# The start of a retention and feed-forward kernel: v scaled by ScalarE, weight conversion behind the rows, fewer warm-up matmuls

## The chip, the cores and the metric

The kernel runs on one core of a Trainium2 chip. Its time is device time of that core in microseconds (us), the median of several runs of the same program. The trace is one more execution, taken by the hardware profiler. TensorE does the matmuls, VectorE and ScalarE elementwise work, GpSimd (POOL in the rows) a few tensor operations, SyncE (SP) issues nearly all transfers.

## The reference

A retention layer and a feed-forward layer, in float32:

```python
state = zeros(B, H, D, D)                     # B 4, H 8, S 768, D 64
for t in range(S):
    state = gamma * state + k[t] (outer) v[t] # gamma: one decay per head
    y[t] = scale * q[t] @ state
x = y as (3072 tokens, 512)
h = x @ w_in                                  # 512 x 2048
g = h * clip(h + 3, 0, 6) / 6
out = g @ w_out                               # 2048 x 512
```

## The kernel before

**Tiling.** The 3072 tokens are 24 row slices (`NROW`) of 128 tokens, six per batch; four slices (`UR`) make a unit of 512 tokens, so there are six units. The recurrence over t is done in slices: scores k·q of a slice, masked to be causal, times v, plus the running state times q. The decay is taken out by scaling v with one constant per token and head (`cst_sb`) and y with its reciprocal (`dq`).

**A row burst** (`burst(r)`) is one visit of that part. On TensorE: `y` of slice r-1 from the state (L218), scores `sc` of slice r (L225), `y` of slice r-1 from the masked scores (L229), running sum `uz` of slice r (L253). On VectorE: `xr` (y times decay, L244), the mask `am` of the scores (L266). On ScalarE: the copy `state` of `uz` (L262). Then `x`, the feed-forward input, is split into a high half (ScalarE, L127) and a low half (VectorE, L128), since a product is made of three reduced-precision matmuls high·high, high·low, low·high. The score bank, the `y` bank and the mask tile exist once, so bursts follow each other closely: the next scores wait for the mask, the next `y` for `xr`.

**Weights.** w_in and w_out come as 64-bit words and are turned into float32 by integer operations (`to_f32`, L99 to L124): L109, L110, L115, L118, L121 on VectorE and L113 on ScalarE, 512 columns at a time, and then the same split in two halves. A staging tile `st` exists twice; the other temporaries (`we`, `wb`, `ww`) once. In `attention()` the first eight slices (`AHEAD`) are loaded ahead, and after slices 0, 1, 4 and 7 (`WITH`) one of 16 w_in blocks is loaded and converted (`build_w1`). Blocks 4 to 15 follow later, one per product.

**Products.** `mm1(u, jj)` computes 12 matmuls `h` (L309), then `g` on ScalarE (L313) and VectorE (L314), which goes to HBM. The steps run through unit 0 with unit 1 between, then units 2 to 5; between the first products the next bursts stand. After that the second product (L395) reads `g` back.

**What sets the order.** All engines run their instructions in the order in which they stand. On TensorE that order is written out in the program (`tc.manual_schedule`). On the others a scheduler places instructions by readiness and by where they stand in the program text, so moving a call moves its instructions on VectorE, ScalarE and SyncE's transfer queue. Eight transfers are under way at a time; a ninth waits for the first to land.

**The start.** `WARM` = 24 matmuls on a zero tile run first (L170). The table that ScalarE needs for its functions is loaded ahead of its first activation, that of the first conversion. v of a slice is scaled by one GpSimd instruction (L196), which waits for v to land.

Of the kernel before, what the change touches and what calls it, by code (L numbers as in the profile page):

```python
# [9 lines left out]
F32 = mybir.dt.float32  # L10
# [3 lines left out]
I64 = mybir.dt.int64  # L14
AF = mybir.ActivationFunctionType
ALU = mybir.AluOpType
# [3 lines left out]
P = 128  # L20
# [9 lines left out]
def retention_ffn(ctx: ExitStack, tc: tile.TileContext, qkv, w_in, w_out, dvs, dqs, out, B, H, S, D):  # L30
# [6 lines left out]
    nc = tc.nc  # L37
# [4 lines left out]
    NK = DM // P  # L42
# [3 lines left out]
    UT = UR * P  # L46
    NU = NROW // UR
    HM = DM // 2
    WARM = 24
    AHEAD = 2 * UR  # L50
    WITH = (0, 1, 4, 7)
    BUFS = {"lkt": 1, "lqt": 2, "lvn": 2, "lkn": 1}
    SPARE = ("lkn", "lkt", "lqt", "lqt")
    BLK = 2 * P
# [19 lines left out]
    )  # L74
    ebias = const.tile([P, 1], F32, name="ebias")
    nc.gpsimd.memset(ebias, -896.0 * 2**23)
    serial = iter(range(1 << 30))

    def nm(s):
        return f"{s}_{next(serial)}"  # L80
# [15 lines left out]
    ps_a = att.enter_context(tc.tile_pool(name="ps_a", bufs=1, space=PSUM, side="right"))  # L96


    def to_f32(src):  # L99

        n = src.shape[-1]
        st = wst.tile([P, n], I64, tag="st", name=nm("st"), bufs=2)
        b = wst.tile([P, n], I32, tag="wb", name=nm("wb"))
        e = wst.tile([P, n], I32, tag="we", name=nm("we"))
        w = wst.tile([P, n], F32, tag="ww", name=nm("ww"))
        nc.sync.dma_start(out=st, in_=src)
        words = st.bitcast(I32).rearrange("p (n w) -> p n w", w=2)
        lo, hi = words[:, :, 0], words[:, :, 1]
        nc.vector.tensor_scalar(out=e, in0=hi, scalar1=0x7FF00000, scalar2=None, op0=ALU.bitwise_and)  # L109
        nc.vector.tensor_scalar(  # L110
            out=b, in0=hi, scalar1=0xFFFFF, scalar2=0x100000, op0=ALU.bitwise_and, op1=ALU.bitwise_or
        )
        nc.scalar.activation(out=e, in_=e, func=AF.Relu, scale=8.0, bias=ebias)  # L113
        y = b.bitcast(F32)
        nc.vector.scalar_tensor_tensor(  # L115
            out=y, in0=lo.bitcast(U32), scalar=2.0**-32, in1=b, op0=ALU.mult, op1=ALU.add
        )
        nc.vector.scalar_tensor_tensor(  # L118
            out=e, in0=hi, scalar=-2147483648, in1=e, op0=ALU.bitwise_and, op1=ALU.bitwise_or
        )  # L120
        nc.vector.scalar_tensor_tensor(  # L121
            out=w, in0=y, scalar=2.0**-20, in1=e.bitcast(F32), op0=ALU.mult, op1=ALU.mult
        )
        return w  # L124
# [11 lines left out]
            w1s[s] = wpool.tile([P, 14, 2, P], F32R, tag="w", name=nm("w1"))  # L136
        return w1s[s], o

    def build_w1(j):
        w = to_f32(w_in[j]).rearrange("p (k n) -> p k n", k=NK)  # L140
        k = 0
        while k < NK:
            t, o = w1_block(j, k)
            n = min(NK - k, 14 - o)
            split(t[:, o : o + n, 0], t[:, o : o + n, 1], w[:, k : k + n])
            k += n
# [4 lines left out]
    def build_w2(n):  # L151
        j, h = divmod(n, 2)
        if not h:
            w2c[j] = wpool.tile([P, 7, 2, 2, P], F32R, tag="w", name=nm("w2"))
        w = to_f32(w_out[j, h]).rearrange("p (b n) -> p b n", b=4)
        sm = wst.tile([P, 4, P], F32, tag="ws", name=nm("ws"))
        m12, m11, m21, m22 = (w[:, i] for i in range(4))
        dve_sub(sm[:, 1], m12, m11)
        dve_sub(sm[:, 2], m22, sm[:, 1])
        dve_sub(sm[:, 3], m22, m12)  # L160
        dve_sub(sm[:, 0], sm[:, 2], m21)
        split(w2c[j][:, 0:3, 0, h], w2c[j][:, 0:3, 1, h], w[:, 1:4])
        split(w2c[j][:, 3:7, 0, h], w2c[j][:, 3:7, 1, h], sm)
# [14 lines left out]
    def load(r):  # L178

        t = rows[r] = {}
        if r < AHEAD and r % 2 == 0:
            early[r] = wpool.tile([P, 7, NPAIR, P], F32, tag="w", name=nm("early"))
        for i, (x, n) in enumerate((("kt", 1), ("qt", 0), ("vn", 3), ("kn", 2))):
            o = r % 2 * 4 + i
            if r < AHEAD and o < 7:
                t[x] = early[r // 2 * 2][:, o]
            else:  # L190
                tag = SPARE[r // 2] if r < AHEAD else f"l{x}"
                t[x] = apool.tile([P, NPAIR, P], F32, tag=tag, name=nm(x), bufs=BUFS[tag])
            if x != "kn" or r % ROWS_B < ROWS_B - 1:
                nc.sync.dma_start(out=t[x].rearrange("p h n -> p (h n)"), in_=qkv[r, n])
        v = t["vn"].rearrange("p a (h e) -> p (a h) e", h=2)
        nc.gpsimd.tensor_tensor(  # L196
            out=v, in0=v, in1=cst_sb[:, r % ROWS_B, :, None].to_broadcast([P, H, D]), op=ALU.mult
        )

    def load_decay(r):  # L200
        if r < AHEAD:
# [70 lines left out]

    def attention():

        for r in range(AHEAD):
            load(r)
            load_decay(r)
            if r in WITH:
                build_w1(WITH.index(r))
        for r in range(NROW + 1):  # L280
            if r == AHEAD:
                burst(r, new=False)
                yield
                burst(r, old=False)
            else:
                burst(r)
            if r >= AHEAD - 1 and r + 1 < NROW:
                load(r + 1)
            if AHEAD <= r < NROW:
                load_decay(r)  # L290
            yield
# [194 lines left out]
```

## Time and profile before

| | |
|---|---|
| median of 3 runs | 618.72 us (616.77 to 618.96) |
| profiled execution | 617.5 us, its span 615.8 us |
| TensorE busy | 598.9 us (97%) |
| VectorE busy | 459.6 us (75%) |
| ScalarE busy | 242.0 us (39%) |
| GpSimd busy | 26.2 us (4%) |
| mean granted TensorE clock | 0.989 |

The span runs from the first to the last instruction of the trace; the profiled time includes what lies around it. A share of the span is an average: TensorE's 97% says nothing of the first 43 us, in which it works 31.56 us. So the front has to be read from timelines, in which a row is one instruction or several equal ones in a row: its start, its time, the engine, the line, output and inputs by the program's names, their shapes, the count, and in brackets how long the engine had nothing to do before it and what ended that. A float32 matmul stands as two records there: 48 for the 24 of the warm-up. The granted clock is 1.00 at TensorE's full 2.4 GHz and 0.50 at 1.2 GHz.

### The profile page before, as it was taken

To read this page: it belongs to the slowest core of one execution; us is meant where nothing else is said; L and a number is where in the kernel's file an instruction comes from. 1 tells how busy PE (TensorE), PEld (TensorE's weight loads), DVE (VectorE), ACT (ScalarE), POOL (GpSimd) and SP (SyncE) were. 2 spreads that over 40 slices of the span, in tenths; PEclk is the share of its full clock that TensorE was granted. 3 is DMA by queue.
4 is the path that set the end of the run, shared out by engine and by line. 5 is a ranking of instruction groups with operands and counts; after the bars stand their busy time and mean duration, and the time that the engine had idled before them with its cause. 6 is when DMAs were issued, how large, how long until landed. Compare 5 with 4: busy or idle time off the path is not lost.

```text
span 615.8 us, 11512 instructions
## 1 busy us (share of the span) xinstructions
PE 598.9 (97%) x4464; PEld 541.1 (88%) x4464; DVE 459.6 (75%) x960; ACT 242.0 (39%) x475; POOL 26.2 (4%) x32
## 2 busy tenths in 40 slices
PE   7779999999999999999999999999999999999997
PEld 7658788888788888888888889999999999999997
DVE  4669999999633399333335997988998889888993
ACT  2224454453322253222223554444444444444441
POOL 1301000000000100000000000000000000000000
PEclk9779999999999999999999999999999999999999
DMA  8936577765754457544425435434443444434421
GB/s 325 388 126 211 189 256 237 236 213 174 251 215 157 157 187 238 189 155 155 154 85 188 139 119 188 137 106 141 146 147 117 134 137 137 138 103 137 138 70 35
DMA packets 64726, 104.06 MB, mean 169 GB/s; under 512 B 5792, under 2 KB 30880, under 8 KB 64672
## 3 DMA queue, kind: packets, MB, share of 16 engines
q1 hardware_dynamic: 64528, 103.31, 49.8%
q8 instruction: 35, 0.57, 0.4%
q14 instruction: 19, 0.16, 0.1%
q10 hardware_dynamic: 144, 0.02, 0.0%
HBM read 71.85 MB, written 31.46 MB: 168 GB/s over the span
## 4 chain that ended last, share of the span: by engine, by line
PE 78%; DVE 18%; issue 3%; ACT 1%; DMA 0%; DVEq 0%; ACTq 0%
PE o L395 39%; PE h L309 30%; PE sc L225 3%; DVE g L314 3%; PE y L229 2%; DVE we L118 2%; DVE am L266 2%; DVE wb L115 2%; DVE w L128 2%; PE y L218 2%; DVE ww L121 2%; PE idle L170 1%; DVE x L128 1%; DVE we L109 1%; DVE xr L244 1%
## 5 line engine op out<-in xcount | busy, mean ns | idle before, releaser
L309 PE MATMUL h<-x,w 128*128 128x512 f32 x1152 | 271.6, 395 | 5.6 <-ACT x L127 4.2
L309 PEld LDWEIGHTS h<-x,w 128*128 128x128 f32 x1152 | 215.9, 189 | 53.9 <-ACT x L127 4.8
L395 PEld LDWEIGHTS o<-w,gc 128*128 128x128 f32 x2016 | 239.4, 190 | 0.1
L395 PE MATMUL o<-w,gc 128*128 128x256 f32 x2016 | 239.5, 281 | 0.0
L314 DVE SCALAR_TENSOR_TENSOR g<-g,h 128x512 f32<-128x512 f32 x96 | 65.6, 684 | 89.7 <-ACT g L313 89.7
L313 ACT ACTIVATE g<-h,three 128x512 f32<-128x512 f32 x96 | 65.6, 685 | 110.4 <-PE h L309 105.8
L127 ACT ACTIVATE gc<-gr 128x256 fp32r<-128x256 f32 x144 | 49.6, 407 | 117.2 <-PE o L395 113.9
L128 DVE TENSOR_TENSOR gc<-gr,gc 128x256 fp32r<-128x256 f32 x144 | 52.7, 420 | 19.7 <-ACT gc L127 19.6
L128 DVE TENSOR_TENSOR gc<-gsum,gc 128x768 fp32r<-128x768 f32 x96 | 62.0, 688 | 5.6 <-ACT gc L127 5.6
L127 ACT ACTIVATE gc<-gsum 128x768 fp32r<-128x768 f32 x96 | 54.5, 616 | 0.1
L127 ACT ACTIVATE w<-ww 128x384 fp32r<-128x384 f32 (+2 forms) x34 | 18.7, 555 | 50.2 <-DVE ww L121 45.1
L113 ACT ACTIVATE we<-we,ebias 128x512 int32<-128x512 int32 x32 | 22.9, 717 | 16.8 <-DVE we L109 16.8
L266 DVE TENSOR_TENSOR am<-sc,mask 128x1024 f32<-128x1024 f32 x24 | 29.2, 1215 | 0.4 <-PE sc L225 0.4
L196 POOL TENSOR_TENSOR vn<-vn,cst_sb 128x512 f32<-128x512 f32 x16 | 16.9, 1059 | 250.3 <-DMA vn<-in_qkv 250.3
L121 DVE SCALAR_TENSOR_TENSOR ww<-wb,we 128x512 f32<-128x512 f32 x32 | 24.3, 758 | 0.7
L118 DVE SCALAR_TENSOR_TENSOR we<-st,we 128x512 int32<-128x512 int32 x32 | 24.0, 750 | 0.0
L262 ACT ACTIVATE state<-uz 128x512 f32<-128x512 f32 x20 | 11.8, 590 | 27.6 <-PE uz L253 27.6
L128 DVE TENSOR_TENSOR w<-ww,w 128x384 fp32r<-128x384 f32 (+2 forms) x34 | 20.2, 598 | 2.8 <-ACT w L127 2.8
L115 DVE SCALAR_TENSOR_TENSOR wb<-st,wb 128x512 f32<-128x512 uint32 x32 | 22.0, 686 | 0.2
L86 DVE TENSOR_TENSOR gsum<-gr 128x256 f32<-128x256 f32 x48 | 20.4, 424 | 1.7 <-DMA gr<-gd 0.3
L83 DVE TENSOR_TENSOR gsum<-gr,gsum 128x256 f32<-128x256 f32 x48 | 20.2, 421 | 0.7
L244 DVE TENSOR_TENSOR xr<-y,dq 128x512 f32<-128x512 f32 x16 | 11.0, 688 | 12.5 <-PE y L229 12.5
(49 smaller groups left out, 379.2 us busy)
## 6 DMA issues: line engine op xcount, KB each, us to landing
gd<-g SPq DMA_DIRECT2D x96, 256.0 KB, 2.1
gr<-gd SPq DMA_DIRECT2D x96, 256.0 KB, 3.1
st<-in_w_in SPq DMA_DIRECT2D x16, 512.0 KB, 3.7
st<-in_w_out SPq DMA_DIRECT2D x16, 512.0 KB, 3.8
early<-in_qkv SPq DMA_DIRECT2D x28, 256.0 KB, 6.0
out<-ot SPq DMA_DIRECT2D x11, 512.0 KB, 2.8
kn<-in_qkv SPq DMA_DIRECT2D x16, 256.0 KB, 4.9
kt<-in_qkv SPq DMA_DIRECT2D x16, 256.0 KB, 4.5
```

The source lines that it names most:

```text
L86: nc.vector.tensor_tensor(out=out_, in0=a, in1=b, op=ALU.add)
L113: nc.scalar.activation(out=e, in_=e, func=AF.Relu, scale=8.0, bias=ebias)
L115: nc.vector.scalar_tensor_tensor(out=y, in0=lo.bitcast(U32), scalar=2.0**-32, in1=b, op0=ALU.mult, op1=ALU.add)
L118: nc.vector.scalar_tensor_tensor(out=e, in0=hi, scalar=-2147483648, in1=e, op0=ALU.bitwise_and, op1=ALU.bitwise_or)
L121: nc.vector.scalar_tensor_tensor(out=w, in0=y, scalar=2.0**-20, in1=e.bitcast(F32), op0=ALU.mult, op1=ALU.mult)
L127: nc.scalar.activation(out=hi, in_=src, func=AF.Copy)
L128: nc.vector.tensor_tensor(out=lo, in0=src, in1=hi, op=ALU.subtract)
L266: nc.vector.tensor_tensor(out=new["am"].rearrange("p h a n -> p (h a) n"), in0=sc.rearrange("p h a n -> p (h a) n"), in1=mask[:, None, :]. ...
L309: nc.tensor.matmul(h, t[:, o, a], xs[u][b][:, k], start=k + n == 0, stop=(k, n) == (NK - 1, 2), skip_group_check=True)
L313: nc.scalar.activation(out=g, in_=h, func=AF.Relu, bias=three)
L314: ins = nc.vector.scalar_tensor_tensor(out=g, in0=g, scalar=6.0, in1=h, op0=ALU.min, op1=ALU.mult)
L395: nc.tensor.matmul(ps, gc[:, a, LEFT[i], jj, :], wc[:, RIGHT[i], b_], start=first and j == 0 and n == 0, stop=j == NFP - 1 and n == 2, ski ...
```

## The change

Four things change, all in the first part of the program:

- `WARM` goes from 24 to 14.
- A one-column activation on ScalarE stands at the start, so that its table load does too.
- For the first eight slices v is scaled by ScalarE, with eight instructions of 64 columns (one per head), instead of one GpSimd instruction of 512. Later slices stay on GpSimd.
- Loading and converting a w_in block are parted (`fetch`, `to_f32`). The first four blocks are fetched after slices 0, 2, 3 and 5 and converted behind the bursts of slices 0, 2, 3 and 4.

```diff
-    WARM = 24
+    WARM = 14
     AHEAD = 2 * UR
-    WITH = (0, 1, 4, 7)
+    WITH = (0, 2, 3, 5)
...
+    table = const.tile([P, 1], F32, name="table")
+    nc.scalar.activation(out=table, in_=three, func=AF.Relu, bias=three)
...
-    def to_f32(src):
-        n = src.shape[-1]
-        st = wst.tile([P, n], I64, tag="st", name=nm("st"), bufs=2)
+    def fetch(src):
+        st = wst.tile([P, src.shape[-1]], I64, tag="st", name=nm("st"), bufs=2)
+        nc.sync.dma_start(out=st, in_=src)
+        return st
+    def to_f32(st):
+        n = st.shape[-1]
         b = wst.tile([P, n], I32, tag="wb", name=nm("wb"))
         e = wst.tile([P, n], I32, tag="we", name=nm("we"))
         w = wst.tile([P, n], F32, tag="ww", name=nm("ww"))
-        nc.sync.dma_start(out=st, in_=src)
...
-    def build_w1(j):
-        w = to_f32(w_in[j]).rearrange("p (k n) -> p k n", k=NK)
+    def build_w1(j, st=None):
+        w = to_f32(fetch(w_in[j]) if st is None else st).rearrange("p (k n) -> p k n", k=NK)
...
-        nc.gpsimd.tensor_tensor(
-            out=v, in0=v, in1=cst_sb[:, r % ROWS_B, :, None].to_broadcast([P, H, D]), op=ALU.mult
-        )
+        if r < AHEAD:
+            for h in range(H):
+                nc.scalar.activation(
+                    out=v[:, h], in_=v[:, h], func=AF.Copy, scale=cst_sb[:, r % ROWS_B, h : h + 1]
+                )
+        else:
+            nc.gpsimd.tensor_tensor(
+                out=v, in0=v, in1=cst_sb[:, r % ROWS_B, :, None].to_broadcast([P, H, D]), op=ALU.mult
+            )
...
+        st = []
         for r in range(AHEAD):
             load(r)
             load_decay(r)
             if r in WITH:
-                build_w1(WITH.index(r))
+                st.append(fetch(w_in[len(st)]))
         for r in range(NROW + 1):
...
                 burst(r)
+            if st and r in (0, 2, 3, 4):
+                build_w1(len(WITH) - len(st), st.pop(0))
```

VectorE's first twelve instructions behind the two memsets, in the kernel before (L109 to L121: conversion, `w1` L128: low half of weights, `am` L266: mask, `xr` L244 and `x` L128: a slice's output and its low half):

```order
L109 TENSOR_SCALAR we_4_139<-st_2_137 128x512
L110 TENSOR_SCALAR wb_3_138<-st_2_137 128x512
L115 SCALAR_TENSOR_TENSOR wb_3_138<-st_2_137,wb_3_138 128x512
L266 TENSOR_TENSOR am_29_258<-sc_27_239,mask_75 128x1024
L118 SCALAR_TENSOR_TENSOR we_4_139<-st_2_137,we_4_139 128x512
L121 SCALAR_TENSOR_TENSOR ww_5_140<-wb_3_138,we_4_139 128x512
L128 TENSOR_TENSOR w1_6_148<-ww_5_140,w1_6_148 128x4x128
L109 TENSOR_SCALAR we_10_160<-st_8_158 128x512
L110 TENSOR_SCALAR wb_9_159<-st_8_158 128x512
L244 TENSOR_TENSOR xr_33_279<-y_30_260,early_1_135 128x512
L115 SCALAR_TENSOR_TENSOR wb_9_159<-st_8_158,wb_9_159 128x512
L118 SCALAR_TENSOR_TENSOR we_10_160<-st_8_158,we_10_160 128x512
```

The same place in the changed kernel (lines 6 to 15 higher: mask L278, `xr` L256, low halves L134, conversion L115 to L127):

```order
L115 TENSOR_SCALAR we_17_261<-st_2_136 128x512
L278 TENSOR_TENSOR am_15_258<-sc_13_239,mask_75 128x1024
L116 TENSOR_SCALAR wb_16_260<-st_2_136 128x512
L124 SCALAR_TENSOR_TENSOR we_17_261<-st_2_136,we_17_261 128x512
L121 SCALAR_TENSOR_TENSOR wb_16_260<-st_2_136,wb_16_260 128x512
L127 SCALAR_TENSOR_TENSOR ww_18_262<-wb_16_260,we_17_261 128x512
L256 TENSOR_TENSOR xr_23_291<-y_20_272,early_1_134 128x512
L278 TENSOR_TENSOR am_25_305<-sc_21_273,mask_75 128x1024
L134 TENSOR_TENSOR x_22_290<-xr_23_291,x_22_290 128x4x128
L256 TENSOR_TENSOR xr_28_329<-y_26_307,early_1_134 128x512
L278 TENSOR_TENSOR am_30_343<-sc_27_312,mask_75 128x1024
L134 TENSOR_TENSOR x_22_290<-xr_28_329,x_22_290 128x4x128
```

The mask now stands behind the conversion's first instruction instead of its third, the second conversion has left this place for the two following slices, and the low half of the first weights has gone behind the fourth `x`. One instruction of the first conversion is still ahead of every mask.

ScalarE ahead of the first product, in the kernel before (`state` L262, high halves L127, `we` of a conversion L113, first `g` L313):

```order
L127 ACTIVATE x_32_278<-xr_43_355 128x4x128
L113 ACTIVATE we_17_194<-we_17_194,ebias_78 128x512
L127 ACTIVATE w1_6_148<-ww_18_195 128x4x128
L262 ACTIVATE state_49_405<-uz_125 128x512
L127 ACTIVATE x_32_278<-xr_48_393 128x4x128
L313 ACTIVATE g_52_422<-h_51_409,three_73 128x512
```

In the changed kernel (`state` L274, high halves L133, `we` L119, scaling of v L204, of slices 5 and 6 here):

```order
L274 ACTIVATE state_45_439<-uz_117 128x512
L133 ACTIVATE x_22_290<-xr_44_427 128x4x128
L204 ACTIVATE early_8_184<-early_8_184,cst_sb_71 128x64 x8
L133 ACTIVATE w1_19_269<-ww_18_262 128x4x128
L133 ACTIVATE w1_19_269<-ww_33_347 128x4x128
L119 ACTIVATE we_40_395<-we_40_395,ebias_78 128x512
L204 ACTIVATE early_11_213<-early_11_213,cst_sb_71 128x64 x8
L133 ACTIVATE w1_19_269<-ww_41_396 128x4x128
```

The high half of the first weights, which the first `h` reads, now stands behind the fourth `x` and the eight instructions that wait for v of slice 5; those of the second and third weights follow it.

## Rows read from the trace of the kernel before

**Rows 1.** Stages: length, busy us (count) per engine, PEclk, DMA share, GB/s.
```profile
70.00:158.00 88.00, 87.90 (x556) 73.22 (x554) 86.90 (x168) 43.50 (x73) 3.26 (x3) 1.00 0.67 226
158.00:612.00 454.00, 453.71 (x3375) 418.82 (x3375) 321.69 (x714) 176.09 (x366) 11.60 (x11) 1.00 0.44 146
```

**Rows 2.** TensorE's timeline: start, us, instruction, count, idle before and releaser.
```profile
1.25 7.58 PE L170 MATMUL idle<-warm 128*128 128x128 f32 x48 [1.25 <-DVE warm L167]
...
11.32 1.16 PE L225 MATMUL sc<-early 64*128 64x128 f32 x16 [0.79 <-DVE am L266]
...
20.09 2.08 PE L225 MATMUL sc<-early 64*128 64x128 f32 x16 [3.23 <-DVE am L266]
...
27.50 1.09 PE L229 MATMUL y<-am,early 128*64 128x128 f32 x16
...
36.81 0.79 PE L309 MATMUL h<-x,w 128*128 128x512 f32 x1 [3.64 <-ACT x L127]
38.08 5.02 PE L309 MATMUL h<-x,w 128*128 128x512 f32 x11 [0.47 <-DVE x L128]
...
46.03 3.02 PE L309 MATMUL h<-x,w 128*128 128x512 f32 x12
...
67.81 2.79 PE L309 MATMUL h<-x,w 128*128 128x512 f32 x11 [0.50 <-DVE x L128]
```

**Rows 3.** VectorE's timeline, 8 to 68 us.
```profile
8.15 0.43 DVE L109 TENSOR_SCALAR we<-st 128x512 int32<-128x512 int32 x1 [6.36 <-DMA st<-in_w_in]
...
10.04 1.23 DVE L266 TENSOR_TENSOR am<-sc,mask 128x1024 f32<-128x1024 f32 x1 [0.40 <-PE sc L225]
11.18 1.08 DVE L118 SCALAR_TENSOR_TENSOR we<-st,we 128x512 int32<-128x512 int32 x1
...
13.68 0.69 DVE L128 TENSOR_TENSOR w<-ww,w 128x512 fp32r<-128x512 f32 x1 [0.70 <-ACT w L127]
...
24.12 0.69 DVE L244 TENSOR_TENSOR xr<-y,early 128x512 f32<-128x512 f32 x1 [3.25 <-PE y L229]
...
28.64 0.69 DVE L244 TENSOR_TENSOR xr<-y,early 128x512 f32<-128x512 f32 x1 [1.77 <-PE y L229]
...
32.84 1.53 DVE L118 SCALAR_TENSOR_TENSOR we<-st,we 128x512 int32<-128x512 int32 x1
...
43.85 0.69 DVE L314 SCALAR_TENSOR_TENSOR g<-g,h 128x512 f32<-128x512 f32 x1 [5.83 <-ACT g L313]
...
45.86 0.69 DVE L118 SCALAR_TENSOR_TENSOR we<-st,we 128x512 int32<-128x512 int32 x1
...
67.07 0.68 DVE L128 TENSOR_TENSOR x<-xr,x 128x512 fp32r<-128x512 f32 x1
```

**Rows 4.** GpSimd's timeline: scaling of v.
```profile
5.69 1.04 POOL L196 TENSOR_TENSOR early<-early,cst_sb 128x512 f32<-128x512 f32 x1 [4.29 <-DMA early<-in_qkv]
10.67 1.04 POOL L196 TENSOR_TENSOR early<-early,cst_sb 128x512 f32<-128x512 f32 x1 [3.94 <-DMA early<-in_qkv]
...
32.75 1.06 POOL L196 TENSOR_TENSOR early<-early,cst_sb 128x512 f32<-128x512 f32 x1 [1.66 <-DMA early<-in_qkv]
```

**Rows 5.** ScalarE's groups by form, whole run: busy us, mean ns, idle before.
```profile
L127 ACT ACTIVATE gc<-gr 128x256 fp32r<-128x256 f32 x144 | 49.6, 407 | 117.2 <-PE o L395 113.9 <-DMA gr<-gd 3.4
L127 ACT ACTIVATE gc<-gsum 128x768 fp32r<-128x768 f32 x48 | 39.9, 831 | 0.1
L113 ACT ACTIVATE we<-we,ebias 128x512 int32<-128x512 int32 x32 | 22.9, 717 | 16.8 <-DVE we L109 16.8
...
L127 ACT ACTIVATE w<-ww 128x512 fp32r<-128x512 f32 x14 | 8.8, 632 | 23.7 <-DVE ww L121 21.0 <-issue 2.6
```

**Rows 6.** ScalarE's timeline: table load, two copies in a row.
```profile
8.66 1.28 ACT L113 ACT_TABLE_LOAD   x1 [8.66 <-DVE we L109]
...
47.30 0.73 ACT L127 ACTIVATE w<-ww 128x256 fp32r<-128x256 f32 x2 [1.67 <-DVE ww L121]
```

**Rows 7.** One stage of the front, columns as in rows 1.
```profile
20.00:24.00 4.00, 3.91 (x36) 3.69 (x38) 0.87 (x2) 0.00 (x0) 1.36 (x2) 0.50 1.05 394
```

More of the change, by code (lines that the diff above doesn't have):

```diff
@@ L154, in build_w2 @@
             w2c[j] = wpool.tile([P, 7, 2, 2, P], F32R, tag="w", name=nm("w2"))
-        w = to_f32(w_out[j, h]).rearrange("p (b n) -> p b n", b=4)
+        w = to_f32(fetch(w_out[j, h])).rearrange("p (b n) -> p b n", b=4)
         sm = wst.tile([P, 4, P], F32, tag="ws", name=nm("ws"))
```

## Prediction

> **What bounds the kernel now.** I read the stage table first. From 70 to 158 us TensorE is busy 87.90 of 88.00 us, from there to 612 us 453.71 of 454.00 [rows 1]: however the front is ordered, the matmuls behind it run without a hole, so time can only come from when that stream starts. VectorE is full from 70 to 158 us too (86.90 of 88.00). So a lead at 70 us lasts to the end only if both engines have it: the smaller of the two counts.
>
> TensorE's timeline shows the stream's start [rows 2]: 24 warm-up matmuls hold the engine from 1.25 to 8.83 us, row bursts with holes follow, the first product `h` starts at 36.81 us (after 3.64 us without work) and goes on at 38.08, and a last hole ends at 67.81, where a low half of `x` is awaited from VectorE. VectorE's timeline says why [rows 3]: its first conversion waits for `w_in` until 8.15 us; idle times of 0.40, 0.70, 3.25, 1.77 and 5.83 us follow, the last for the first `g`; and the fourth `x` low half of the second unit, the one TensorE waits for, begins at 67.07 and ends at 67.75. That end is the milestone that I work with.
>
> A second loss hides in VectorE's busy time. `L118` takes 0.69 us undisturbed; at 11.18 it took 1.08 and at 32.84 it took 1.53, each time ending about 0.55 us after a GpSimd scaling of v that had begun at 10.67 and 32.75 [rows 3, 4]. These are the first and the last of five such instructions from 8 to 38 us; with the three between them (16.16, 19.96 and 30.38 us) the excesses are 0.39, 0.84, 0.23, 0.57 and 0.84, together 2.9 us.
>
> **The change, part by part.** Up to the milestone VectorE executes the same instructions, in another order. From 8.15 to 67.75 are 59.6 us; less 11.95 us of the idle above and 2.9 us of blocking, 44.7 us of work remain. The milestone's new time is 8.15 + 44.7 + what the new order leaves idle, so I walk through that order.
>
> *Warm-up.* 14 of 24 at the old mean is 14/24 x 7.58 = 4.4 us: the end moves from 8.83 to 5.7 us. The first scores need `kt` and `qt`, which are queued ahead of v, and v had landed when GpSimd took it at 5.69 [rows 4]; so they run from 5.7 to 6.9. That alone gives little: VectorE's new first instruction still waits for `w_in` until 8.15, and the first mask stands behind it, at 8.5 instead of 10.04.
>
> *Scaling of v.* Eight ScalarE instructions of 128x64 per row, which no row shows. A copy of 128x256 takes 407 ns and one of 128x768 831 ns, so 0.83 ns a column, and 64 columns make 248 ns [rows 5]. The form with a bias read from memory takes 717 against 632 ns for 512 columns, 85 ns more; I add that for the scale read from memory: 0.33 us. Two copies in a row took 0.73 us for 2 x 0.41, an overlap of 0.09 [rows 6]. Eight are 8 x 0.33 - 7 x 0.09 = 2.0 us. Lower end: without the 85 ns, 1.35 us. Upper end: each as long as the 128x256 copy, without overlap, 3.3 us. I take 2.0, since each part of it is a measured difference; GpSimd needed 1.04. The Trainium skill, "ScalarE: Activation LUTs", section "What ACT_TABLE_LOAD costs", gives 186 ns + 0.833 ns per column, 93 ns more for a pointer operand and 93 ns of overlap; by that the eight would take 2.0 us, and the sum would stay.
>
> *Table.* Its load took 1.28 us from 8.66 [rows 6], while VectorE had its own second and third instruction to do; now it is over before v lands. I put it at 0: the activation behind it now waits for VectorE's first instruction (8.5) and is done by 9.7, and its result is asked for at 10.0.
>
> *Transfers.* They go on at about 390 GB/s [rows 7], 0.67 us for a tile of 256 KB and 1.3 for 512 KB. From v of row 1 at 10.67, by the new order of the queue: v of row 2 at 14.0, row 3 at 18.7, row 4 at 23.3, row 5 at 26.7, row 6 at 30.7, row 7 at 33.4. The third and fourth `w_in` wait for a staging buffer inside the queue, now ahead of more rows; VectorE frees these at about 11.3 and 22.0, before the queue gets there (about 15 and 22.6). So the price is nothing, and each microsecond that the second is late beyond 0.6 delays rows 6 and 7 by one.
>
> *Rows 0 to 4.* A row's cycle is scores 1.16, y 1.09, xr 0.69, mask 1.23 us, less overlaps, about 4.05 [rows 2, 3]. `xr` of row 0 at 12.0. ScalarE scales v of row 1 until 12.65, the state sums end at 13.3, scores of row 2 start at 14.3; `xr` of row 1 at 16.45 (before 24.12), of row 2 at 20.45 (before 28.64), of row 3 at 25.4; fourth `x` low half done at 27.8. VectorE's idle: 0.6 (for ScalarE's high half), 1.4, 0.35, 0.35 and 1.65 us, 4.35 together.
>
> *First product.* It needs the high half of the first weights, and in ScalarE's new order that stands behind v of row 5: landed 26.7, scaled until 29.15, high half until 29.75. VectorE stands idle for 1.95 us, and `h` starts at 29.8 instead of 36.81. From here VectorE goes through three weight conversions before its first `g`, which fills the place of the 5.83 us. ScalarE's scaling of rows 6 and 7 (32.3 to 34.25, 35.6 to 37.6) costs it some 0.2 us of waits. Idle in all 6.5 us.
>
> *Sum.* 8.15 + 44.7 + 6.5 = 59.35, a lead of 8.4 us against 67.75. Placing each instruction by hand behind what it waits for gives 58.7, a lead of 9.0, because some of the 44.7 is latency that now lies inside waits. I take 8.7. TensorE has it too: `h` at half clock, as before, until about 35.4, then bursts and products of about 3 us each [rows 2], and the matmul that stood at 67.81 could start at 58.85. The profiled execution took 617.5 us (span 615.8): 608.8. It lies 1.2 below the runs' median of 618.72, so for a median 610.0.
>
> **Rivals.** *One more slow spell of TensorE.* The granted clock was 0.50 (1.2 GHz) from 20 to 24 us [rows 7], after a hole of 3.23 us, and the matmuls after the hole of 3.64 were slow again: 11 in 5.02 us against 12 in 3.02 [rows 2]. The holes of the new front before 26 us are at most 1.45 us (8.3 to 9.75), but there are several between 6.9 and 12.6. In a slow spell the scores cost 0.92 us more (2.08 against 1.16 [rows 2]) and y about as much, 1.8 per row; for some 7 us, 1.7 rows: 3.0 us, 613.0. For it speaks that less warm-up lies ahead; against it that both spells of the trace followed holes over 3 us, and the hole of 0.79 at 11.32 none. The Trainium skill, "TensorE: Matmul & The Clock Gate", section "What's actually happening", says that the monitor is free-running and isn't reset by a kernel; by that the same holes may fall well in one run and badly in another, which no run here shows yet.
>
> *ScalarE becomes the bound.* With 3.3 us per row it has those, 0.6 each for state and `x`, and every second row 0.72 us to do in a cycle of 4.05: about 0.8 late on four rows, 1.3 on row 5 ahead of the first product, 2.5 on rows 6 and 7: 7.0 us lost, 617.0. For it: one engine in order, waiting for each v, with state and `x` queued behind. Against it: the rows give 0.33 us for such an instruction. The Trainium skill, "ScalarE: Activation LUTs", section "Rules for kernel authors", would keep multiplications off ScalarE; this rival is what that would look like here.
>
> *The clock stays low (slower than before).* If TensorE stays at 1.2 GHz from the end of the warm-up to the first product, five rows cost 1.8 us each, 9.0 us, and the lead is used up. From there it decides: one more burst and product at half speed cost about 3 us each, 625. For it: only 4.4 us of warm-up, and a front made of short bursts. Against it: after both spells of the trace full speed came back while the bursts still had holes or one product ran.
>
> **How the numbers follow.** Forecast 64% (own range 608 to 612: 1.35 us for the scaling gives 1.2 us more, a late transfer or wait takes 1 to 2 away). One more slow spell 18% (611 to 614.5). ScalarE bound 12%. Clock low 6%. 0.5% is 3.1 us, about what a measurement can tell: below 615.6 is faster, 64 + 18 = 82%; the same 12%; slower 6%. The range 606.5 to 614.5 holds the first two, with 1.5 us below for waits that I counted and that may vanish.
>
> **What would show it.** Right: first mask at about 8.5; eight scalings in about 2.0 us; the first weights' high half directly behind v of row 5 near 29; `h` near 30; no VectorE wait over 1 us between that and the milestone near 59; TensorE full from there. Wrong: scalings over 0.4 us each, granted clock 0.50 before 26 us, a hole in TensorE or VectorE after 60 us that gives the lead back.

## The result, and the profile after

The changed kernel took 610.39 us (median of 4 runs, 609.93 to 610.87); the kernel before, on the same chip, 617.75 us (4 runs, 616.1 to 618.96). The ratio is 0.9883, 95% interval 0.9853 to 0.9912: 7.4 us faster, where 610.0 us was forecast. The profiled execution took 610.77 us.

TensorE's timeline of the changed kernel (start, us, instruction, count, idle before and what ended it):

```profile
1.24 6.23 PE L176 MATMUL idle<-warm 128*128 128x128 f32 x28 [1.24 <-DVE warm L173]
7.40 1.16 PE L237 MATMUL sc<-early 64*128 64x128 f32 x16
...
19.39 1.16 PE L237 MATMUL sc<-early 64*128 64x128 f32 x16 [0.53 <-DVE x L134]
...
30.82 4.66 PE L324 MATMUL h<-x,w 128*128 128x512 f32 x12 [3.66 <-ACT w L133]
...
60.76 2.79 PE L324 MATMUL h<-x,w 128*128 128x512 f32 x11 [0.51 <-DVE x L134]
```

The first `h` starts at 30.82 instead of 36.81, and the matmul behind the last hole at 60.76 instead of 67.81 [rows 2]: a lead of 7.05 us. The stages (length, busy us of TensorE, its weight load, VectorE, ScalarE and GpSimd, granted clock, DMA share, GB/s) show that it is kept:

```profile
61.00:150.00 89.00, 89.00 (x562) 74.49 (x562) 87.90 (x171) 43.12 (x72) 3.73 (x3) 1.00 0.66 221
150.00:604.00 454.00, 453.55 (x3370) 418.53 (x3369) 321.87 (x713) 177.14 (x368) 11.71 (x11) 1.00 0.44 147
20.00:24.00 4.00, 3.52 (x50) 3.02 (x47) 2.82 (x5) 3.60 (x11) 0.00 (x0) 1.00 1.05 389
31.20:34.40 3.20, 3.20 (x9) 2.27 (x8) 3.13 (x7) 2.14 (x7) 0.00 (x0) 0.50 0.69 253
```

From 61 to 604 us TensorE has 0.45 us of holes (0.39 from 70 to 612 us before [rows 1]). The stretch from 20 to 24 us, at half clock before [rows 7], is at full clock; one slow spell is left, under the first `h`.

VectorE's timeline from its first conversion to the milestone (the fourth low half of `x` in the second unit), all its waits and the instructions that the text speaks of:

```profile
9.01 0.43 DVE L115 TENSOR_SCALAR we<-st 128x512 int32<-128x512 int32 x1 [7.23 <-DMA st<-in_w_in]
9.35 1.22 DVE L278 TENSOR_TENSOR am<-sc,mask 128x1024 f32<-128x1024 f32 x1
...
12.85 0.69 DVE L256 TENSOR_TENSOR xr<-y,early 128x512 f32<-128x512 f32 x1
...
16.96 0.69 DVE L256 TENSOR_TENSOR xr<-y,early 128x512 f32<-128x512 f32 x1 [1.65 <-PE y L241]
...
21.63 0.69 DVE L256 TENSOR_TENSOR xr<-y,early 128x512 f32<-128x512 f32 x1 [0.84 <-PE y L241]
22.63 0.69 DVE L124 SCALAR_TENSOR_TENSOR we<-st,we 128x512 int32<-128x512 int32 x1 [0.31 <-ACT we L119]
...
26.75 0.69 DVE L256 TENSOR_TENSOR xr<-y,early 128x512 f32<-128x512 f32 x1 [1.69 <-PE y L241]
...
30.80 0.69 DVE L134 TENSOR_TENSOR w<-ww,w 128x512 fp32r<-128x512 f32 x1 [1.64 <-ACT w L133]
...
43.19 1.54 DVE L121 SCALAR_TENSOR_TENSOR wb<-st,wb 128x512 f32<-128x512 uint32 x1
...
45.85 0.93 DVE L127 SCALAR_TENSOR_TENSOR ww<-wb,we 128x512 f32<-128x512 f32 x1
...
60.02 0.69 DVE L134 TENSOR_TENSOR x<-xr,x 128x512 fp32r<-128x512 f32 x1
```

The waits sum to 6.13 us against 12.19 before: the 11.95 that the prediction counts [rows 3] and one of 0.24 that it leaves out:

```profile
26.18 0.69 DVE L128 TENSOR_TENSOR x<-xr,x 128x512 fp32r<-128x512 f32 x1 [0.24 <-ACT x L127]
```

The wait of 5.83 for the first `g` is gone, and from 30.80 to the milestone there is none. ScalarE's timeline:

```profile
1.23 1.28 ACT L79 ACT_TABLE_LOAD   x1 [1.23 <-PEq L484]
...
6.17 2.02 ACT L204 ACTIVATE early<-early,cst_sb 128x64 f32<-128x64 f32 x8 [3.36 <-DMA early<-in_qkv]
...
28.25 2.00 ACT L204 ACTIVATE early<-early,cst_sb 128x64 f32<-128x64 f32 x8
30.16 0.61 ACT L133 ACTIVATE w<-ww 128x512 fp32r<-128x512 f32 x1
```

The table load now ends before v lands [rows 6]. Eight scalings take 2.02 us. The high half of the first weights runs right behind those of slice 5.

### The profile page after: what moved, and what is told of

Read it like the earlier page. It is cut to its first block, busy times and chain, and to the rows that moved or that the text cites. A ratio compares the mean times of both kernels' runs of the same rounds, so it can differ in the third digit from the quotient of the medians.

```text
span 609.0 us, 11521 instructions
## 1 busy us (share of the span) xinstructions
PE 594.9 (98%) x4444; PEld 537.4 (88%) x4444; DVE 457.5 (75%) x960; ACT 257.6 (42%) x540; POOL 18.5 (3%) x24
## 4 chain that ended last, share of the span: by engine, by line
PE 75%; DVE 17%; DMA 3%; issue 2%; ACT 2%; SPq 0%; DVEq 0%; ACTq 0%
PE o L410 39%; PE h L324 30%; DMA early<-in_qkv 3%; DVE g L329 3%; PE y L241 2%; PE sc L237 2%; DVE w L134 2%; DVE wb L121 2%; DVE ww L127 2%; DVE we L124 2%; PE y L230 1%; DVE am L278 1%; DVE we L115 1%; DVE ws L86 1%; DVE wb L116 1%
## 5 line engine op out<-in xcount | busy, mean ns | idle before, releaser
L133 ACT ACTIVATE gc<-gr 128x256 fp32r<-128x256 f32 x144 | 49.6, 407 | 117.0 <-PE o L410 114.2
L134 DVE TENSOR_TENSOR gc<-gr,gc 128x256 fp32r<-128x256 f32 x144 | 52.7, 421 | 20.2 <-ACT gc L133 20.2
L134 DVE TENSOR_TENSOR gc<-gsum,gc 128x768 fp32r<-128x768 f32 x96 | 62.1, 689 | 5.5 <-ACT gc L133 5.5
L133 ACT ACTIVATE gc<-gsum 128x768 fp32r<-128x768 f32 x96 | 54.6, 616 | 0.1
L133 ACT ACTIVATE w<-ww 128x384 fp32r<-128x384 f32 (+2 forms) x34 | 18.7, 555 | 43.4 <-DVE ww L127 40.9
L278 DVE TENSOR_TENSOR am<-sc,mask 128x1024 f32<-128x1024 f32 x24 | 29.2, 1216 | 0.0
L119 ACT ACTIVATE we<-we,ebias 128x512 int32<-128x512 int32 x32 | 22.9, 715 | 12.7 <-DVE we L115 12.7
L134 DVE TENSOR_TENSOR w<-ww,w 128x384 fp32r<-128x384 f32 (+2 forms) x34 | 20.7, 615 | 3.8 <-ACT w L133 3.8
L127 DVE SCALAR_TENSOR_TENSOR ww<-wb,we 128x512 f32<-128x512 f32 x32 | 23.0, 719 | 0.7
L121 DVE SCALAR_TENSOR_TENSOR wb<-st,wb 128x512 f32<-128x512 uint32 x32 | 22.8, 714 | 0.2
L124 DVE SCALAR_TENSOR_TENSOR we<-st,we 128x512 int32<-128x512 int32 x32 | 21.9, 685 | 0.3 <-ACT we L119 0.3
L274 ACT ACTIVATE state<-uz 128x512 f32<-128x512 f32 x20 | 11.8, 591 | 22.9 <-PE uz L265 22.9
L256 DVE TENSOR_TENSOR xr<-y,dq 128x512 f32<-128x512 f32 x16 | 11.0, 689 | 12.5 <-PE y L241 12.5
```

What stands on the lines that cost most here:

```text
L121: nc.vector.scalar_tensor_tensor(out=y, in0=lo.bitcast(U32), scalar=2.0**-32, in1=b, op0=ALU.mult, op1=ALU.add)
L124: nc.vector.scalar_tensor_tensor(out=e, in0=hi, scalar=-2147483648, in1=e, op0=ALU.bitwise_and, op1=ALU.bitwise_or)
L127: nc.vector.scalar_tensor_tensor(out=w, in0=y, scalar=2.0**-20, in1=e.bitcast(F32), op0=ALU.mult, op1=ALU.mult)
L133: nc.scalar.activation(out=hi, in_=src, func=AF.Copy)
L134: nc.vector.tensor_tensor(out=lo, in0=src, in1=hi, op=ALU.subtract)
L278: nc.vector.tensor_tensor(out=new["am"].rearrange("p h a n -> p (h a) n"), in0=sc.rearrange("p h a n -> p (h a) n"), in1=mask[:, None, :]. ...
```

## Experiments

Theories at the start: the *waits theory* (the gain is the idle time that the new order takes from VectorE), the *GpSimd theory* (it is the blocking, GpSimd's instructions lengthening VectorE's, that ends when GpSimd no longer scales v) and the *clock theory* (it is the slow spells, stretches in which TensorE's granted clock is at 0.50, that go). All kernels were timed in five rounds, each batch beside the kernel before, whose medians were 617.0 to 617.9 us. The table collects them; the rows are quoted where a verdict rests on them.

| kernel | first conversion | first `h` | last hole ends | median us | ratio (95%) |
|---|---|---|---|---|---|
| before | 8.15 | 36.81 | 67.81 | 617.75 | |
| changed | 9.01 | 30.82 | 60.76 | 610.39 | 0.9883 (0.9853 to 0.9912) |
| order_only | 9.07 | 28.94 | 59.78 | 609.42 | 0.9872 (0.9859 to 0.9884) |
| scale_only | 7.93 | 33.48 | 64.27 | 614.17 | 0.9940 (0.9926 to 0.9954) |
| warm14_only | 9.32 | 33.98 | 65.81 | 614.65 | 0.9948 (0.9936 to 0.9961) |
| before_filled | 8.87 | 34.29 | 62.58 | 613.58 | 0.9932 (0.9920 to 0.9944) |
| gp_scaling | 8.29 | 28.48 | 60.05 | 610.23 | 0.9879 (0.9860 to 0.9899) |
| scale_five | 9.06 | 29.31 | 61.01 | 610.60 | 0.9887 (0.9868 to 0.9905) |
| after_warm24 | 8.44 | 30.81 | 62.11 | 612.15 | 0.9912 (0.9894 to 0.9930) |
| late_w | 12.04 | 31.68 | 63.55 | 613.43 | 0.9931 (0.9914 to 0.9949) |
| w_first | 4.51 | 30.49 | 60.09 | 610.47 | 0.9884 (0.9867 to 0.9901) |
| w_first_gp | 4.54 | 28.08 | 59.11 | 609.38 | 0.9872 (0.9853 to 0.9890) |
| split67 | 8.58 | 28.65 | 59.59 | 610.50 | 0.9893 (0.9876 to 0.9909) |
| w_first_split67 | 4.49 | 27.95 | 58.96 | 609.05 | 0.9866 (0.9852 to 0.9881) |

In all fourteen rows the median less the end of the last hole is 548.8 to 551.0 us, and the profiled execution's own time less it 549.4 to 550.4: whatever is done to the front, the rest costs the same, and the place of that one matmul predicts the time to about 1 us. The columns in the middle are from one profile of each kernel.

**The order alone** (fetch and conversion parted and moved; GpSimd scales v, 24 warm-up matmuls, no early table), against the kernel before:

```diff
-    WITH = (0, 1, 4, 7)
+    WITH = (0, 2, 3, 5)
...
-                build_w1(WITH.index(r))
+                st.append(fetch(w_in[len(st)]))
...
+            if st and r in (0, 2, 3, 4):
+                build_w1(len(WITH) - len(st), st.pop(0))
```

> The kernel before with the new order alone: w_in fetched after slices 0, 2, 3, 5 and converted behind the bursts; v still scaled by GpSimd, 24 warm-up matmuls, no early table load. Waits theory (the gain is VectorE's idle time of the front, and it counts where its order puts it): fourth x low half of the second unit written at about 60 us, time about 610.5 us, 7 us below before, though GpSimd blocks again. GpSimd theory (the gain is the blocking of 2.9 us that goes with GpSimd's scaling): 2.9 us of the gain missing, about 613.3 us. Clock theory (the gain is the second slow spell of TensorE that the new kernel does not have): 610.5 if one spell is left, 614 or more if two.

609.42: the whole gain, with all of GpSimd's scalings still there. The GpSimd theory falls as the main cause. The waits theory's 610.5 stands, 1.1 us off; VectorE's waits up to the milestone sum to 4.25 us against 12.19. One slow spell is left, under the first `h`, and for that the clock theory gave 610.5 too: this run does not part the two. TensorE's timeline of it:

```profile
28.94 5.03 PE L316 MATMUL h<-x,w 128*128 128x512 f32 x12 [1.79 <-ACT w L131]
...
59.78 2.79 PE L316 MATMUL h<-x,w 128*128 128x512 f32 x11 [0.51 <-DVE x L132]
```

**ScalarE's scaling alone**, in the kernel before:

```diff
+        if r < AHEAD:
+            for h in range(H):
+                nc.scalar.activation(out=v[:, h], in_=v[:, h], func=AF.Copy, scale=cst_sb[:, r % ROWS_B, h : h + 1])
+        else:
             nc.gpsimd.tensor_tensor(
```

> The kernel before with ScalarE's scaling of the first eight v alone (the table load comes first by itself); old order, 24 warm-up matmuls. Waits theory, by a walk through VectorE's order: first x chain some 4 to 5 us earlier, the wait of 5.8 us for the first g stays, about 613 us. GpSimd theory: 617.7 - 2.9 = 614.8 us. Clock theory: 617.7 if both slow spells stay, 614 if one goes.

614.17, 3.1 us below the kernel before in that batch (617.22), between the waits theory's 613 and the GpSimd theory's 614.8. Both have a part: of the milestone's lead of 3.5 us about 1.4 are waits (10.75 us for 12.19) and 1.6 blocking. VectorE's row shows that the wait for the first `g` stays, shorter than the 5.83 of before [rows 3]:

```profile
39.64 0.69 DVE L320 SCALAR_TENSOR_TENSOR g<-g,h 128x512 f32<-128x512 f32 x1 [4.07 <-ACT g L319]
```

**14 warm-up matmuls alone**, in the kernel before:

```diff
-    WARM = 24
+    WARM = 14
```

> The kernel before with 14 warm-up matmuls instead of 24 and nothing else. The scheduler puts VectorE's instructions in another order because of it: the first mask ahead of the conversion's third instruction, the first xr and the second mask ahead of the second conversion's multiplications. Waits theory: second mask at about 15.5 instead of 18.8 us, rows some 4 us earlier, the wait for the first g stays, about 613 us. GpSimd theory: 617.7, since all blocking stays. Clock-stays-low rival: slower than 618 us, granted clock 0.50 in the rows.

614.65, 2.6 us below. The rival in which the clock then stays low falls, and so does the GpSimd theory's 617.7; the waits theory's 613 is missed by 1.6. The number of warm-up matmuls also acts through the scheduler, which here puts the first mask ahead of the conversion's third instruction. The wait for the first `g` is as long as before:

```profile
41.99 0.69 DVE L314 SCALAR_TENSOR_TENSOR g<-g,h 128x512 f32<-128x512 f32 x1 [5.79 <-ACT g L313]
```

**The clock held up**: the kernel before with 12 matmuls on a zero tile in each of TensorE's two long holes (VectorE, ScalarE and the queue keep their order):

```diff
+        if r == 2:
+            fill(12)
...
+        if (u, jj) == (0, 0):
+            fill(12)
```

> The kernel before with idle matmuls in the two holes of TensorE (12 ahead of the scores of the third slice, 12 ahead of the first product); VectorE's, ScalarE's and SyncE's order is the same as before. If the clock holds: clock theory 611 us (all the gain). Waits theory: the slow spells are on the chain only where VectorE waits for TensorE (24.12 and 43.85 us), worth about 2 us each at most, 614 us. GpSimd theory: 617.7, no change.

613.58. The stage row shows a mean granted clock of 1.00 up to 60 us (columns as above):

```profile
0.00:60.00 60.00, 54.30 (x568) 48.16 (x569) 43.80 (x69) 20.12 (x33) 12.08 (x19) 1.00 0.77 277
```

So the two slow spells cost the kernel before 3.6 us (617.22 in that batch), between what the waits theory (614) and the clock theory (611) gave, nearer the first. They act through the waits: with the clock held, VectorE's sum to 7.84 us instead of 12.19, 1.67 where 3.25 stood and 3.60 where 5.83 stood. The clock theory falls as the whole cause; about half of the gain can be had through it alone. Order, scaling, warm-up and clock each bring 2.6 to 7.8 us by themselves, the first three together (with the early table) 7.4: they relieve the same holes and don't add.

**The changed kernel with v scaled by GpSimd** (that part of the change undone):

> The changed kernel with only the scaling of v put back on GpSimd (early table, 14 warm-up matmuls and the new order stay). Changed kernel: 610.4. Waits theory (the gain is VectorE's idle time that the order removes; ScalarE's scaling stands ahead of the first weights' high half and costs there what GpSimd's blocking would): first h near 29, VectorE's hole ahead of the first weights' low half (1.64 us) mostly gone, two or three blockings of 0.4 to 0.8 us instead, 609 to 610. GpSimd theory (the scaling on ScalarE is worth its own 2 to 3 us): 612.5 to 613.5, milestone (the low half of x that the last hole of TensorE waits for) near 63.

610.23, the same as the changed kernel. So moving the scaling to ScalarE, as part of this change, brought nothing. VectorE's rows show the exchange:

```profile
10.70 1.53 DVE L121 SCALAR_TENSOR_TENSOR wb<-st,wb 128x512 f32<-128x512 uint32 x1
...
16.98 0.69 DVE L250 TENSOR_TENSOR xr<-y,early 128x512 f32<-128x512 f32 x1 [1.65 <-PE y L235]
...
19.66 1.27 DVE L116 TENSOR_SCALAR wb<-st 128x512 int32<-128x512 int32 x1
...
26.27 0.69 DVE L250 TENSOR_TENSOR xr<-y,early 128x512 f32<-128x512 f32 x1 [1.69 <-PE y L235]
...
32.43 1.53 DVE L124 SCALAR_TENSOR_TENSOR we<-st,we 128x512 int32<-128x512 int32 x1
...
35.20 1.15 DVE L115 TENSOR_SCALAR we<-st 128x512 int32<-128x512 int32 x1
```

The blockings are back (1.53 for 0.69, 1.27 for 0.42 and so on), but waits are down to 1.65 and 1.69 us, 3.34 together against 6.13. Of the 2.8 us more in the changed kernel, 1.64 for the first weights' high half and 0.31 are for ScalarE's scaling of v, which the awaited instruction stands behind. The third, 0.84 ahead of the `xr` at 21.63, is not: that `xr` needs v of slice 2, scaled by 16.5. TensorE came later there, because its scores of slice 3 started at 19.39 and here at 18.92:

```profile
18.92 1.16 PE L231 MATMUL sc<-early 64*128 64x128 f32 x16
```

The row at 19.39 names an `x` that the scores don't read; the transfers of slice 3 were later too (its v is taken at 19.96, here at 19.53), and they are the likelier cause. In this kernel a blocked instruction (1.27 us at 19.66) stood in that place.

**ScalarE scales slices 0 to 4 only**, so that the high half no longer stands behind v of slice 5:

```diff
-        if r < AHEAD:
+        if r < 5:
```

> The changed kernel with ScalarE scaling v for slices 0 to 4 only, 5 to 7 on GpSimd, so that the first weights' high half no longer stands behind v of slice 5. Waits theory: first h near 29 instead of 30.8, VectorE's hole of 1.64 us gone, up to three blockings by GpSimd (0.4 to 0.8 us each) take some of it back: 609 to 610. Rival (the first product is not what the later VectorE chain hangs on): h earlier but the milestone unchanged near 60.7, 610.4.

610.60: the rival. `h` starts 1.5 us earlier and VectorE's wait of 1.64 is gone, but the last hole ends at 61.01. VectorE's waits are 4.70 us for 6.13, and its work is 1.6 us more (47.19 for 45.57), as GpSimd's blocking is back:

```profile
29.31 0.49 PE L324 MATMUL h<-x,w 128*128 128x512 f32 x1 [1.76 <-ACT w L133]
...
61.01 2.79 PE L324 MATMUL h<-x,w 128*128 128x512 f32 x11 [0.51 <-DVE x L134]
```

**The changed kernel with 24 warm-up matmuls**:

> The changed kernel with 24 warm-up matmuls instead of 14; the scheduler then puts the first mask behind the conversion's third instruction again. Waits theory: the first mask about 1.1 us later (near 10.5), but VectorE does conversion work in that time, so nothing is lost: 609.5 to 610.5. Rival (fewer warm-up matmuls are worth their 3 us because the rows start earlier): 612 to 613.5. Clock theory (a longer warm-up keeps TensorE at full speed longer): the one slow spell of the changed kernel stays where it is, near 31 to 34.5, since it follows the hole ahead of the first h: no change from that.

612.15, 1.8 us above the changed kernel, outside what the waits theory gave and inside the rival's 612 to 613.5. But the loss does not come the rival's way: the rows start 1.1 us later (first scores at 8.48 for 7.40), yet the first `h` starts at 30.81, as in the changed kernel (30.82). VectorE begins earlier (8.44), but has nine waits, 8.92 us in all, 2.1 of them behind the first `h`, where the changed kernel has none. Two of those that ScalarE ends:

```profile
22.24 0.69 DVE L134 TENSOR_TENSOR x<-xr,x 128x512 fp32r<-128x512 f32 x1 [1.41 <-ACT x L133]
...
35.39 0.69 DVE L124 SCALAR_TENSOR_TENSOR we<-st,we 128x512 int32<-128x512 int32 x1 [1.22 <-ACT we L119]
```

The second comes from the scheduler's order on ScalarE: `we` stands behind the scaling of slice 6 here, in the changed kernel ahead of it (32.79, the scaling at 33.41).

```profile
32.74 2.00 ACT L204 ACTIVATE early<-early,cst_sb 128x64 f32<-128x64 f32 x8
34.65 0.71 ACT L119 ACTIVATE we<-we,ebias 128x512 int32<-128x512 int32 x1
```

With 24 matmuls and GpSimd (the order alone) it was 609.42. So how the warm-up and the scaling are combined matters more than either: the number of warm-up matmuls moves the scheduler's order, and ScalarE's slower scaling is then waited for.

**The first block fetched after slice 1**:

```diff
-    WITH = (0, 2, 3, 5)
+    WITH = (1, 2, 3, 5)
```

> The changed kernel with the first w_in block fetched after slice 1 instead of slice 0. Transfers theory (part of the 1.7 us that the lead fell short of the forecast was the first 512 KB transfers in front of the rows): v of slice 1 lands about 1.3 us earlier (near 9.8 instead of 11.0), the first mask no longer stands behind a conversion that waits for its block and comes near 8.5, xr of slice 1 near 16, milestone 0.5 to 1.3 us earlier: 609.2 to 610. Rival (VectorE's work is the bound and its first conversion starting 1.3 us later is lost for good): 610.4 to 611.7.

613.43: my theory was wrong, and worse than its rival had it. The mask came at 7.50, but the conversion behind it holds VectorE until its block lands, and TensorE's third scores wait for the second mask, which stands behind that conversion:

```profile
7.50 1.23 DVE L278 TENSOR_TENSOR am<-sc,mask 128x1024 f32<-128x1024 f32 x1 [5.71 <-issue]
12.04 0.43 DVE L115 TENSOR_SCALAR we<-st 128x512 int32<-128x512 int32 x1 [3.31 <-DMA st<-in_w_in]
...
15.72 1.22 DVE L278 TENSOR_TENSOR am<-sc,mask 128x1024 f32<-128x1024 f32 x1
```

```profile
16.99 2.08 PE L237 MATMUL sc<-early 64*128 64x128 f32 x16 [2.38 <-DVE am L278]
```

A slow spell follows that hole (2.08 us for scores that take 1.16 at full clock), so part of the 3.0 us lost against the changed kernel is the clock's.

**The first block fetched ahead of all slices**:

```diff
-    WITH = (0, 2, 3, 5)
+    WITH = (-1, 2, 3, 5)
...
-        st = []
+        st = [fetch(w_in[0])]
```

> The changed kernel with the first w_in block fetched ahead of all slices; VectorE's order stays but for the first conversion, which then stands wholly ahead of the first mask. Changed kernel: 610.4 us, its VectorE begins its first conversion at 9.0. Account theory (the end follows VectorE's chain: start of the first conversion + its work + its idle time up to the milestone, the low half of x that TensorE's last hole waits for): the start moves to about 5, the first mask to about 8.0, about 2.6 us of conversion work stand ahead of it in time that was idle, so 4 us are to be had; rows are then held by their transfers, which I put at half: milestone near 58.7, 608 to 609. Rival (the rows are bound by transfers, VectorE's idle time grows by what its start gains): milestone near 60.7, 610.4. Rival on the other side (slice 0 is later by the 512 KB ahead of it, TensorE gets a hole over 2 us and one more slow spell): 612 to 613.

610.47, the time of the rival that gives all of it back. VectorE starts at 4.51 instead of 9.01, and its waits grow from 6.13 to 10.13 us:

```profile
4.51 0.43 DVE L115 TENSOR_SCALAR we<-st 128x512 int32<-128x512 int32 x1 [2.73 <-DMA st<-in_w_in]
...
8.51 1.23 DVE L278 TENSOR_TENSOR am<-sc,mask 128x1024 f32<-128x1024 f32 x1 [1.18 <-PE sc L237]
12.02 0.69 DVE L256 TENSOR_TENSOR xr<-y,early 128x512 f32<-128x512 f32 x1 [2.29 <-PE y L241]
...
16.14 0.69 DVE L256 TENSOR_TENSOR xr<-y,early 128x512 f32<-128x512 f32 x1 [1.69 <-PE y L241]
```

The cycle of a slice holds here first: from the first `xr` to the second are 4.1 us in both kernels (12.02 to 16.14, and 12.85 to 16.96). At the third the transfers hold, as the rival had it:

```profile
19.06 1.16 PE L237 MATMUL sc<-early 64*128 64x128 f32 x16 [1.02 <-DMA early<-in_qkv]
```

The changed kernel had already put its conversion work into those holes. Of the 4.5 us that the start gains, the milestone keeps 0.7 (60.03 for 60.71).

**The same with GpSimd's scaling**:

> The same with v scaled by GpSimd instead of ScalarE for all slices. Of the changed kernel, undoing the ScalarE scaling left the time as it was (610.2). Account theory: v ready 1 us earlier per slice, where the rows are held by v; GpSimd blocks VectorE by 0.4 to 0.8 us for each slice; with rows held by their transfers the first counts more than the second: 607.5 to 608.5, at most 0.5 from the one with ScalarE. Rival (VectorE is the bound, blocking counts in full): 1 to 2 us above the one with ScalarE.

609.38, 1.1 us below the one with ScalarE: the account's direction, but 1 us above its figure, and the two intervals overlap.

**Both engines share the scaling** (GpSimd slices 0 to 5, ScalarE 6 and 7), without and with the first block ahead:

```diff
-        if r < AHEAD:
+        if 6 <= r < AHEAD:
```

> The changed kernel with GpSimd scaling v of slices 0 to 5 and ScalarE only that of 6 and 7. With all on GpSimd the time was 610.2, with all on ScalarE 610.4. Refined account: up to the first product (near 28.5 us) VectorE waits for the chain of the rows anyway, so GpSimd's blocking costs little there, while ScalarE's scaling of slice 5 puts the first weights' high half 1.6 us back; behind it VectorE is full, so there each blocking (0.85 us for slices 6 and 7) counts and ScalarE's scaling costs nothing. So this should have the better half of both: first h near 28.5, no wait or blocking over 0.5 us on VectorE from there to the milestone but for that of slices 8 and 9, milestone near 58.8, 608.5 to 609.3. Rival (blockings cost nothing here either, the end is set by something else): 610.2.

> The same split of the scaling, with the first w_in block fetched ahead of all slices as well (609.4 with all scaling on GpSimd). Refined account: minus the blockings of slices 6 and 7, about 1.2 us: 608 to 608.7, the fastest kernel here. Rival: 609.4, no change.

610.50 and 609.05, against 610.23 and 609.38 with GpSimd alone: no gain that can be told. The refined account's figures (608.5 to 609.3 and 608 to 608.7) are both missed, and the rivals' 610.2 and 609.4 are nearer. In the first, the blocking's place was taken by a wait of 1.33 us for the first `g`, whose product ran in a slow spell; in the second, GpSimd's scalings of slices 8 and 9 blocked VectorE at 45.36 and 46.64 instead. The second has the lowest median of all kernels, 608.90 to 609.31 in 4 runs; its interval overlaps the changed kernel's, so that it beats it is likely and not settled.

## Why the prediction was right, and where it was not

**The form of the sum held.** Time follows the one milestone, and the milestone is VectorE's start plus its work plus its waits. The last is bookkeeping and true of any engine; what the runs add is that the work hardly changes. Less what blocking lengthens, it is 43.5 to 44.7 us in all fourteen profiles, so start, waits and blocking decide. They are not independent: w_first moved the start by 4.5 us and got 4.0 us of waits for it.

**The lead was mis-sized, and the base hid it by luck.** Forecast was a lead of 8.7 us from a median of 618.72; measured 7.04 (67.75 to 60.71) in the profiles and 7.4 in the medians, from 617.75. All batches put the kernel before 0.8 us or more under 618.72. The base was 1.0 us too high and the lead 1.3 too long, and that these two cancel to within 0.4 us is luck; with the right base the same lead would have given 609.05.

By the steps of the sum, 8.15 + 44.7 + 6.5 = 59.35 became 9.01 + 45.57 + 6.13 = 60.71:

- *Start*, 0.86 late. Nothing ties it to the change: where the first block stands behind slice 0 in the queue, the first conversion began between 7.93 and 9.32 in ten profiles of ten kernels, in the old order (7.93 to 9.32) as in the new (8.29 to 9.07).
- *Work*, 0.87 more. The step "2.9 us of blocking, 44.7 us of work remain" counted the blocking of the first eight slices alone. In the 44.7 there were still the wait of 0.24 and 0.48 us of blocking by slice 8, in the kernel before:

```profile
49.16 1.04 POOL L196 TENSOR_TENSOR vn<-vn,cst_sb 128x512 f32<-128x512 f32 x1 [15.34 <-DMA vn<-in_qkv]
49.59 1.16 DVE L128 TENSOR_TENSOR x<-xr,x 128x512 fp32r<-128x512 f32 x1
```

  Slices 8 and 9 stay on GpSimd, and in the changed kernel they lengthened the rows at 43.19 and 45.85 by 0.85 and 0.24 us, 1.09 where the sum held 0.48. About 0.4 us more is left that no row accounts for. GpSimd's row after:

```profile
43.11 1.07 POOL L208 TENSOR_TENSOR vn<-vn,cst_sb 128x512 f32<-128x512 f32 x1 [41.71 <-DMA vn<-in_qkv]
```

- *Waits*, 6.13 for 6.5: 0, 1.65, 0.84, 0.31, 1.69 and 1.64 where 0.6, 1.4, 0.35, 0.35, 1.65 and 1.95 stood, and none for the 0.2 behind them.
- *The choice* of 8.7 between 8.4 (the sum) and 9.0 (placed by hand) went to the worse side by 0.3.

**Warm-up**: wrong in size, without effect. The mean of rows 2 mixes half and full clock, and 14 run mostly at half clock: 6.23 us instead of 4.4 (5.01 to 6.18 in the other kernels with 14). In the kernel before 12 records ran from 2 to 4 us and 21 from 6 to 8, in the changed kernel 12 from 2 to 4 and 11 from 4 to 6. The granted clock of a stage row does not tell this: the trace's first record of it, of full speed, begins at 5.37 us before and at 7.23 after, and a row shows 1.00 where there is no record. The scores were ready at 8.56, and VectorE's first instruction waited until 9.01 anyway; the mask came at 9.35 (forecast 8.5).

**Scaling**: 2.02 us for the forecast 2.0. The Trainium skill, "ScalarE: Activation LUTs", section "What ACT_TABLE_LOAD costs", gives 2.0 us as an estimate from its figures. Trace and page agree.

**Transfers**: later than forecast. ScalarE took v of slices 3 and 4 as they landed, at 19.96 and 24.61 where 18.7 and 23.3 stood.

**First product**: `h` at 30.82 for 29.8, behind v of slice 5 and the high half at 30.16, as described. But that step mattered less than I thought: with `h` at 28.48 (gp_scaling) the time stayed.

**What each part is worth** the prediction did not get from its sum. It booked the blocking as a gain of its own; beside the run without ScalarE's scaling, the changed kernel has waits of the same 2.8 us in the blocking's place, 1.95 of them behind ScalarE. The order alone carries the gain. Its two halves, where the blocks are fetched and where they are converted, were not run apart, and neither was the early table.

**Rivals.** Behind the warm-up no slow spell came before 26 us. It could have: scale_five, which has the same order on VectorE until its first `g`, had one behind a hole of 2.20 us, with a granted clock of 0.61 from 10.6 to 15 us, and none under the first `h` (1.00 from 29 to 33). What one spell more would cost no run shows alone. ScalarE did not become the bound. The clock rose.

**Open**: what decides whether a hole is followed by a slow spell, and whether the 0.3 to 1 us between the fastest kernels is real.

## What to carry to other kernels

Find the last matmul that waits before the stream runs full, and price a change to the front by the engine that releases it: start, work and waits of that engine alone. Parts of such a change that relieve the same holes do not add, so undo each one from the whole as well as trying it alone: here the order brought the whole gain by itself, undoing the scaling changed nothing, and undoing the shorter warm-up cost 1.8 us. An instruction whose data come late belongs behind the ones that others wait for, since all that stands behind it on its engine is late with it.

## What the runs showed of the hardware

**The same hole, two clocks.** In five kernels the first `h` followed a hole of 1.79 us. TensorE's rows of two of them, gp_scaling and split67, and the stage from 28.5 to 32.5 us of each:

```profile
29.24 3.17 PE L318 MATMUL h<-x,w 128*128 128x512 f32 x11 [0.26 <-DVE x L134]
```

```profile
28.50:32.50 4.00, 3.64 (x15) 2.59 (x16) 3.93 (x8) 1.30 (x3) 0.73 (x2) 1.00 1.05 387
```

```profile
29.59 4.45 PE L324 MATMUL h<-x,w 128*128 128x512 f32 x11 [0.45 <-DVE x L134]
```

```profile
28.50:32.50 4.00, 3.41 (x8) 2.29 (x8) 3.93 (x7) 1.34 (x3) 0.49 (x1) 0.63 1.05 385
```

Full speed (2.4 GHz) in the first, partly 1.2 GHz in the second; order_only and w_first_gp had a slow spell too (11 in 4.36 us in the latter), w_first_split67 none (11 in 3.17). The prediction left this open: the Trainium skill, "TensorE: Matmul & The Clock Gate", section "What's actually happening", has the window of the clock gate free-running and not reset when a kernel starts. By that the same holes may fall well in one run and badly in another; these five agree, though as different programs. VectorE felt the spell through the first `g`, for which it waited 1.33 us (split67), 0.62 (order_only) and 0.39 (w_first_gp); without a spell no row shows such a wait. The five times, 609.05 to 610.50, do not sort by it.

**Blocking also hits instructions with one tensor input.** GpSimd's scaling lengthened `L116` (0.42 to 1.27 us) and `L115` (0.43 to 1.15) in gp_scaling as it did those with two; the mask, which reads its scores from PSUM, stayed at 1.20 to 1.25 in every profile. The Trainium skill, "SBUF — State Buffer", section "🔬 SBUF: two separate sides", has VectorE and GpSimd share a port pair that one of them holds for a whole instruction; that an instruction of 0.69 us which GpSimd's blocks ends 0.55 us behind it (43.11 + 1.07 = 44.18, the end at 44.73) agrees with it.
